# Hash attention and a gated feed-forward on one core: earlier loads, earlier hashes, moves of bits one a slot

## The chip, the cores and the metric

The kernel runs on one core of one Trainium2 chip. The time is the device time of one execution in microseconds. Five engines work side by side, each through its own list of instructions in order: TensorE (PE, and PEld for its weight loads), VectorE (DVE), ScalarE (ACT), GpSimd (POOL) and SyncE (SP), which here only issues transfers. An engine whose next instruction must wait holds everything behind it.

## What is computed

```python
def _attn_ref(q, k, v, proj):                 # q, k, v: (4, 8, 768, 64) f32; proj: (64, 6)
    q_bits = (np.einsum('bhsd,dk->bhsk', q, proj) > 0).astype(np.int64)
    k_bits = (np.einsum('bhsd,dk->bhsk', k, proj) > 0).astype(np.int64)
    q_bucket = np.sum(q_bits * powers, axis=-1)
    k_bucket = np.sum(k_bits * powers, axis=-1)
    mask = q_bucket[:, :, :, None] == k_bucket[:, :, None, :]
    scores = np.where(mask, scale * np.matmul(q, k.transpose(0, 1, 3, 2)), -1000000000.0)
    attn = softmax(scores)                    # written out in the reference
    return np.matmul(attn, v)

def _moe_ref(x, w_gate, w_val, w_out, rms_g): # x: (3072, 512), the heads side by side
    xn = x / np.sqrt(np.mean(x * x, axis=-1, keepdims=True) + 1e-06) * rms_g
    g = xn @ w_gate                           # 512 x 1536
    silu = g * (1.0 / (1.0 + np.exp(-g)))
    return (silu * (xn @ w_val) @ w_out)      # 1536 x 512
```

A query sees the keys whose six sign bits equal its own. The kernel adds the bits to the contraction: rows 64 to 75 of the tile QK hold them, scaled, so that one matmul gives a score that the exp turns into zero wherever bits differ.

## The kernel before

**Tiles.** The 4 batches are cut into 8 windows of 384 queries (window w is half of batch w // 2), the 8 heads into 4 pairs; "(b, hp)" is pair hp of batch b. For each pair the kernel loads q, k and v, turns q and k so that the head's 64 channels lie on partitions, casts them to f16 into QK, hashes them and writes the bits into QK.

**Slots.** The list SLOTS has 192 entries (window, head, third of the keys). One pass of the last loop is a slot: it issues the two score matmuls of the next slot (`scores(s + 1)`, L319, into one of two buffers s_ps), the exp of the next slot (`probs(s + 1)`, L329, on ScalarE), and what the plan holds for slot s. The first 48 slots take windows 0 and 1 in the order of TURNS, six slots a pair: window 0 pair 0, window 1 pair 0, window 0 pair 1, window 1 pair 1, window 0 pair 2, window 0 pair 3, window 1 pair 2, window 1 pair 3. From slot 48 on come the windows 2 to 7, one head after the other, and beside each of them the feed-forward of an earlier window: window 0's from slot 48.

**The plan.** `at(s, f, ...)` puts a piece of work into slot s. Within a slot the order is by rank, then by the order of the calls of `at`: ranks under 3 go ahead of the slot's exp, the others behind it. The order in which pieces are issued is the order on every engine's list.

**Pieces.**
- `load_rows` (L111) loads one of q, k, v of a pair in rows of 1,536 bytes; `load_blocks` (L121) loads k or q of a later pair as four transfers with 128-byte pieces. Both go through SyncE's queue. The ten buffers of the pool L are shared by all loads. `load_w` (L494) and `load_wo` (L500) bring the weights through GpSimd's queue, two halves each.
- `keep_pair(b, hp, i)` is a turn, four for a pair (k and q of each head): three transposes on TensorE (t_ps, L169), a copy on VectorE (L178), and for q a cast on ScalarE straight from the bank (L180). `casts` follows a slot later on GpSimd (L183), two for k and one for q. Batch 0 and the pairs (1,0) and (1,1) go this way. The others are turned by VectorE, `turn_dve` (L193), eight pieces a pair, one a slot.
- `hash_head` (batch 0, heads 0 to 3) and `hash_heads` (a pair): eight small f32 matmuls (d_ps, L209), the signs on VectorE (L216), then moves of the bits into QK: twelve rows of 384 each, eight blocks for a pair. A move is a VectorE copy (L250 for a head, L268 for a pair) or a transfer issued by SyncE (L248, L266). A block has a number t: t = 0 and 1 are k and q of the first half of the queries and keys, t = 2 and 3 those of the second. Pairs (1,2) and later are hashed by `hash_pairs` (L284).
- `attn_out` (rank 4.5, three slots after a pair's last exp): VectorE adds a constant to o_ps, the only buffer of its kind (otmp, L356), takes reciprocals (rcp, L361), GpSimd scales (x, L365) and squares (sq, L377); `sumsq` (L381) six slots later sums on VectorE.
- `norm`, `scale_x`, `turn_x` make the normalised, turned x of a window: ss (L388) on VectorE, ms and rstd (L390, L394) on GpSimd, xn (L399) on VectorE, transposes on TensorE (x_ps, L406) and the product with the gains on VectorE (xnT, L407). For window 0 these stand in slots 39, 41 and 45 to 47, and the first gate matmuls (g_ps, L418) in slot 48.

**When what is due.** A pair's bits and casts must be in QK one slot before its first slot: (0,2) and (0,3) in slots 23 and 29 for window 0, and 35 and 41 for window 1; (1,0) in slot 47, (1,1) in slot 53. In the kernel before, turns, hash and moves of a pair stand like this: (0,2) turns in slots 9, 10, 12, 13, hash in 14; (0,3) in 16, 17, 19, 20, hash in 21; (1,0) in 23, 25, 26, 28, hash in 29; (1,1) in 34, 36, 38, 41, hash in 42. VectorE's four moves of a batch-0 pair follow its signs at once, and so do the three of heads 2 (slot 3) and 3 (slot 7). Pair (1,2) is loaded in slots 29 (v), 31 (k) and 34 (q), and turned from slot 44 on.

Of the kernel before, what the change touches and what calls it, by code (L numbers as in the profile page):

```python
# [43 lines left out]
def kernel(  # L44
# [12 lines left out]
    nc = tc.nc  # L57
# [79 lines left out]
    def t0(b, h, which):  # L137
        hp, hh = divmod(h, 2)
        return T0[b, hp, which][:, hh * HALF : (hh + 1) * HALF]
# [66 lines left out]
    def hash_bank(parts):  # L206
        ps = bank("d_ps", [128, HALF])
        for t, (w, src) in enumerate(parts):
            nc.tensor.matmul(  # L209
                ps[32 * t : 32 * t + 32, :], w, src,  # L210
                start=True, stop=True, tile_position=(0, 32 * t),
            )
        return ps

    def signs(bt, ps, n=128):
        nc.vector.tensor_scalar(  # L216
            out=bt[0:n], in0=ps[0:n], scalar1=thr[0:n], scalar2=scl[0:n],
            op0=ALU.is_gt, op1=ALU.mult,
        )

    def bit_rows(b, h, t):
        return QK[b, h // 2][D:KROWS, h % 2, t * HALF : (t + 1) * HALF]
# [3 lines left out]
    def bits_tile(i):  # L226

        if i % 2 == 0:
            held.append(spool.tile([128, S], FP16, name="bits", bufs=3))
        return held[-1][:, (i % 2) * HALF : (i % 2 + 1) * HALF]  # L230

    def hash_head(h):


        kt, qt = t0(0, h, "k"), t0(0, h, "q")
        ps = hash_bank(
            [(pk[:, 0:32], kt), (pq[:, 0:32], qt), (pk[:, 12:44], kt), (pq[:, 12:44], qt)]
        )
        bt = bits_tile(h)
        signs(bt, ps)  # L240

        def move(movers, t0=0):
            for t, eng in enumerate(movers, t0):
                src = bt[32 * t : 32 * t + 12]
                if eng is nc.scalar:
                    nc.scalar.copy(bit_rows(0, h, t), src)
                elif eng is nc.sync:
                    nc.sync.dma_start(out=bit_rows(0, h, t), in_=src)  # L248
                else:
                    eng.tensor_copy(bit_rows(0, h, t), src)  # L250

        return move

    def hash_heads(b, hp, eng=nc.sync):

        ps = hash_bank(
            [(w[:, 0:32], t0(b, 2 * hp + hh, which))
             for hh in range(2) for w, which in ((pk, "k"), (pq, "q"))]
        )
        bt = bits_tile(0)  # L260
        signs(bt, ps)
        for hh, t in [(0, 2), (1, 2), (0, 0), (0, 1), (1, 0), (1, 1), (0, 3), (1, 3)]:
            p0 = 64 * hh + 32 * (t % 2) + 12 * (t // 2)
            dst, src = bit_rows(b, 2 * hp + hh, t), bt[p0 : p0 + 12]
            if t > 1 or eng is nc.sync:
                nc.sync.dma_start(out=dst, in_=src)  # L266
            else:
                eng.tensor_copy(dst, src)  # L268

    def hash_pairs(b, hps):  # L270

# [272 lines left out]
    def at(s, f, *a, rank=3):  # L544
        plan[s].append((rank, len(plan[s]), lambda: f(*a)))
# [1 line left out]
    def steps(s):  # L547
        return sorted(plan[s], key=lambda e: e[:2])

    def hash_step(h):  # L550
        hash_head(h)((nc.vector, nc.vector, nc.vector, nc.sync))

    for h in range(2):
        at(1 + h, cast_half, 0, h, "q", 1)
        at(h, (bits0, bits1)[h], (nc.vector,), 3)

    for hp, turns, sv in ((1, (1, 2, 4, 5), 8), (2, (9, 10, 12, 13), 19), (3, (16, 17, 19, 20), 25)):
        for i, s in enumerate(turns):
            at(s, keep_pair, 0, hp, i)
            at(s + 1, casts, 0, hp, i)  # L560
        at(sv, v_prep, 0, hp)
    at(3, hash_step, 2)
    at(7, hash_step, 3)
    at(14, hash_heads, 0, 2, nc.vector)
    at(21, hash_heads, 0, 3, nc.vector)
    for hp, s in enumerate((6, 16, 30, 36)):
        at(s, v_mean, 0, hp, 2, range(6))
    for i, (t, src) in enumerate(((wg, moe_w_gate), (wv, moe_w_val))):
        at(2 + 5 * i, load_w, t, src, 0, 768)
        at(13 + 5 * i, load_w, t, src, 768, 1536)  # L570
        at(36 + 5 * i, load_wo, 6 * i, 6 * i + 6)

    for hp, loads, turns, sv in ((0, (9, 11, 16), (23, 25, 26, 28), 30),
                                 (1, (14, 19, 24), (34, 36, 38, 41), 45)):
        for which, s in zip("kqv", loads):
            at(s, load_rows, nc.sync, 1, hp, which)
        for i, s in enumerate(turns):
            at(s, keep_pair, 1, hp, i)  # L580
            at(s + 1, casts, 1, hp, i)
        at(turns[3] + 1, hash_heads, 1, hp)
        at(sv, v_prep, 1, hp)

    work = {
# [121 lines left out]
```

## Time and profile before

| | |
|---|---|
| median of 3 runs | 352.48 us (352.04 to 353.3) |
| the profiled execution | 351.2 us |
| its span, first to last instruction | 349.4 us |
| granted TensorE clock, mean | 0.99 |
| PE busy | 330.6 us (95%) |
| DVE busy | 237.1 us (68%) |
| ACT busy | 209.8 us (60%) |
| POOL busy | 146.6 us (42%) |
| moved by DMA | 31.36 MB, mean 90 GB/s |

The profile lists the time in which each engine was busy, the waits with what ended them, and a chain of work followed back from the last instruction. A busy share is a mean over stages with different limits. This kernel has two: the first 48 slots (about 9.6 to 57 us), in which TensorE makes scores and turns pairs without any feed-forward to fill its time, and the rest. By stretches (us; busy time of each engine, the granted clock, the share of the DMA engines that was busy, GB/s), the first 80 us are:

```profile
core 0: us, PE busy (x) PEld busy (x) DVE busy (x) ACT busy (x) POOL busy (x), PEclk, DMA share, GB/s
0.00:10.00 10.00, 7.87 (x60) 5.78 (x61) 4.78 (x32) 3.49 (x6) 4.17 (x20) 1.00 0.74 231
10.00:20.00 10.00, 9.50 (x96) 5.92 (x96) 7.97 (x19) 8.93 (x14) 7.33 (x12) 1.00 1.11 315
20.00:30.00 10.00, 8.11 (x104) 5.82 (x104) 6.63 (x17) 7.28 (x12) 7.36 (x12) 1.00 1.11 225
30.00:40.00 10.00, 8.41 (x110) 5.83 (x111) 8.52 (x17) 8.73 (x13) 8.58 (x15) 1.00 1.07 263
40.00:50.00 10.00, 9.45 (x124) 6.64 (x125) 5.36 (x12) 9.11 (x14) 8.30 (x14) 1.00 0.18 29
50.00:60.00 10.00, 7.17 (x84) 4.20 (x83) 5.08 (x16) 6.15 (x9) 4.97 (x7) 1.00 1.27 213
60.00:70.00 10.00, 5.48 (x41) 3.10 (x41) 6.15 (x13) 2.85 (x5) 1.64 (x2) 0.66 0.45 68
70.00:80.00 10.00, 10.00 (x87) 5.83 (x86) 8.89 (x21) 5.81 (x10) 4.12 (x5) 1.00 0.90 161
```

Each row says how full the engines are in its ten microseconds, and the third number from the end is the clock that TensorE was granted.

### The profile page before, as it was taken

Reading aid. Unit: us, or ns where it says so; the run is one execution under the profiler, and the core shown is the slowest. Engines: PE = TensorE matmul, PEld = TensorE weight load, DVE = VectorE, ACT = ScalarE, POOL = GpSimd, SP = SyncE. Lnnn points to the kernel's source line nnn. Section 1 sums busy time; section 2 is a strip of 40 time slices with the busy share of each in tenths; the row PEclk is TensorE's granted clock in tenths of the full one; section 3 lists DMA queues with packets and bytes.
Section 4 is the critical chain, followed back from the end, with each engine's and each line's share of the span. In section 5 each row is a group of like instructions: output and inputs, shape, how many; then the busy total and the mean of one; then the engine's idle time right before and its main releaser. Section 6 shows DMA issues by size and latency. Waiting matters only on the chain.

```text
span 349.4 us, 7777 instructions
## 1 busy us (share of the span) xinstructions
PE 330.6 (95%) x2996; PEld 201.7 (58%) x2996; DVE 237.1 (68%) x531; ACT 209.8 (60%) x328; POOL 146.6 (42%) x216
## 2 busy tenths in 40 slices
PE   8898895699999999999999999999999999999995
PEld 6565563356556565566656565566556665555553
DVE  4768663688966797587867797576636663883860
ACT  3888885356566577557766576566767675332331
POOL 4677865143772657621564477513111221110000
PEclk9999999699999999999999999999999999999999
DMA  7999659386284253408345070100010001001002
GB/s 214 350 234 253 139 75 221 50 145 140 43 165 104 57 87 90 106 18 157 73 107 121 16 138 32 62 20 0 19 48 27 3 0 62 32 0 61 32 0 90
DMA packets 80100, 31.36 MB, mean 90 GB/s; under 512 B 65192, under 2 KB 77120, under 8 KB 80064
## 3 DMA queue, kind: packets, MB, share of 16 engines
q1 hardware_dynamic: 76080, 26.09, 30.6%
q0 software_dynamic: 3680, 4.72, 8.3%
q8 instruction: 23, 0.38, 0.5%
q10 hardware_dynamic: 304, 0.07, 0.1%
q14 instruction: 13, 0.11, 0.1%
HBM read 28.32 MB, written 6.29 MB: 99 GB/s over the span
## 4 chain that ended last, share of the span: by engine, by line
PE 82%; DVE 7%; DMA 5%; ACT 3%; issue 1%; SPq 1%; DVEq 0%; ACTq 0%
PE v_ps L428 17%; PE y_ps L442 17%; PE g_ps L418 17%; PE s_ps L319 15%; PE o_ps L341 8%; PE d_ps L209 4%; DMA kL<-in_k_dram 3%; ACT psb L329 2%; PE x_ps L406 1%; DMA qL<-in_q_dram 1%; DVE QK L268 1%; DMA QK<-bits 1%; PE y_ps L666 1%; DVE bits L216 1%; DVE otmp L356 1%
## 5 line engine op out<-in xcount | busy, mean ns | idle before, releaser
L329 ACT ACTIVATE psb<-s_ps 128x768 f16<-128x768 f32 x192 | 150.5, 808 | 31.0 <-PE s_ps L319 29.9
L319 PE MATMUL s_ps<-QK 76*128 76x384 f16 x384 | 93.7, 325 | 4.4 <-ACT psb L329 3.2
L420 ACT ACTIVATE t<-g_ps 128x384 f32<-128x384 f32 x96 | 47.2, 491 | 67.6 <-PE g_ps L418 67.4
L418 PE MATMUL g_ps<-xnT,wg 128*128 128x384 f16 x384 | 78.6, 327 | 7.0 <-DVE xnT L407 7.0
L428 PE MATMUL v_ps<-xnT,wv 128*128 128x384 f16 x384 | 78.7, 327 | 0.4 <-DVE a L430 0.2
L430 DVE SCALAR_TENSOR_TENSOR a<-t,g_ps 128x384 f32<-128x384 f32 x96 | 52.7, 549 | 35.5 <-ACT t L420 33.9
L442 PE MATMUL y_ps<-wo,ht 128*128 128x512 f16 x276 | 69.2, 378 | 0.3 <-DVE a L430 0.3
L365 POOL TENSOR_TENSOR x<-otmp,rcp 128x384 f32<-128x384 f32 x31 | 25.7, 829 | 99.5 <-DVE rcp L361 99.0
L341 PEld LDWEIGHTS <-psb 128*128 128x128 f16 x1152 | 51.9, 97 | 24.2 <-issue 7.4
L431 DVE SCALAR_TENSOR_TENSOR ht<-a,v_ps 128x384 f16<-128x384 f32 x96 | 53.2, 554 | 11.4 <-PE v_ps L428 2.4
L341 PE MATMUL o_ps<-vl,psb 128*128 128x65 f16 x1152 | 56.6, 193 | 1.4 <-DVE otmp L356 1.4
L418 PEld LDWEIGHTS <-wg 128*128 128x128 f16 x384 | 36.0, 97 | 31.2 <-issue 7.6
L428 PEld LDWEIGHTS <-wv 128*128 128x128 f16 x384 | 36.5, 97 | 25.3 <-issue 2.1
L319 PEld LDWEIGHTS <-QK 76*128 76x128 f16 x384 | 31.4, 98 | 22.0 <-issue 8.3
L442 PEld LDWEIGHTS <-ht 128*128 128x128 f16 x276 | 25.8, 97 | 24.1 <-issue 0.5
L449 ACT COPY ysb<-y_ps 128x512 f32<-128x512 f32 x23 | 13.5, 586 | 25.9 <-PE y_ps L442 23.2
L407 DVE TENSOR_TENSOR xnT<-x_ps,gcol 128x512 f16<-128x512 f16 x24 | 16.4, 685 | 15.9 <-PE x_ps L406 15.9
L377 POOL TENSOR_TENSOR sq<-x 128x384 f32<-128x384 f32 x31 | 25.6, 826 | 2.4
L356 DVE TENSOR_TENSOR otmp<-o_ps,cvb 128x390 f32<-128x390 f32 x32 | 17.9, 559 | 11.8 <-PE o_ps L341 11.7
L201 POOL CAST QK<-kT 64x768 f16<-64x768 f32 x20 | 16.4, 821 | 20.0 <-DVE kT L193 12.4
L193 DVE STREAM_TRANSPOSE kT<-kL 128x192 f32<-128x192 f32 x40 | 20.2, 516 | 5.5 <-DMA kL<-in_k_dram 5.5
L201 POOL CAST QK<-qT 64x768 f16<-64x768 f32 x20 | 16.7, 834 | 11.0 <-DVE qT L193 10.4
(74 smaller groups left out, 270.7 us busy)
## 6 DMA issues: line engine op xcount, KB each, us to landing
vL<-in_v_dram SPq DMA_DIRECT2D x16, 384.0 KB
out_dram<-ysb SPq DMA_DIRECT2D x23, 256.0 KB
kL<-in_k_dram SPq DMA_DIRECT2D x40, 96.0 KB
qL<-in_q_dram SPq DMA_DIRECT2D x40, 96.0 KB
kL<-in_k_dram SPq DMA_DIRECT2D x5, 384.0 KB
qL<-in_q_dram SPq DMA_DIRECT2D x5, 384.0 KB
wg<-in_moe_w_gate_dram POOLq DMA_DIRECT2D x2, 768.0 KB, 8.3
wv<-in_moe_w_val_dram POOLq DMA_DIRECT2D x2, 768.0 KB, 9.8
```

What stands on the lines that cost most here:

```text
L201: nc.gpsimd.tensor_copy(QK[b, hp][0:64, hh, o : o + S], T0[b, hp, which][64 * hh : 64 * hh + 64, :])
L319: nc.tensor.matmul(ps[:, j, 0:HALF], k_cols(w // 2, h, 2 * p + j), q_cols(w, h), start=True, stop=True,)
L329: nc.scalar.activation(psb[w, h][:, p], sps.pop(g)[:, :, 0:HALF], AF.Exp, scale=ESCALE,)
L341: nc.tensor.matmul(o[:, c, hh, 0:65], psb[w, h][:, jt // 2, jt % 2, 128 * c : 128 * c + 128], vls[b % 2][:, h, v_chunk(b, h, jt), 0:65], s ...
L365: eng.tensor_mul(xd.rearrange("p c (h d) -> p c h d", h=2), tmp[:, :, :, 0:64], r.to_broadcast([128, 3, 2, 64]),)
L377: nc.gpsimd.tensor_mul(sq, xd, xd)
L418: nc.tensor.matmul(g, wg[:, kt, fs], xnT[w][:, kt], start=(kt == 0), stop=(kt == 3))
L420: nc.scalar.activation(t, g, AF.Tanh, scale=0.5)
L428: nc.tensor.matmul(vv, wv[:, kt, fs], xnT[w][:, kt], start=(kt == 0), stop=(kt == 3))
L430: nc.vector.scalar_tensor_tensor(out=a, in0=t, scalar=1.0, in1=g, op0=ALU.add, op1=ALU.mult)
L431: nc.vector.scalar_tensor_tensor(out=ht[w][:, ft], in0=a, scalar=0.5, in1=vv, op0=ALU.mult, op1=ALU.mult)
L442: nc.tensor.matmul(y, ht[w][:, ft, c * 128 : (c + 1) * 128], wo[:, ft, :], start=(ft == 0), stop=(ft == NF - 1),)
```

## The change

1. Loads: of pair (1,2), k moves from slot 31 to 20, q from 34 to 24, v from 29 to 31; of (1,3), k, q, v from 45, 47, 49 to 36, 40, 46; of (1,0), v from 16 to 15; of (1,1), k, q, v from 14, 19, 24 to 13, 17, 28. Weight loads move by one to three slots, except the first half of the gate.
2. Turns and hashes: (0,2) is turned in slots 8 to 11 and hashed in 13, (0,3) in 13 to 16 and 18, (1,0) in 20, 22, 23, 24 and 26; (1,1)'s hash moves from 42 to 43.
3. Moves of bits: `hash_heads` returns a function that moves given blocks. The batch-0 pairs' odd blocks (t = 2, 3) go to SyncE at once; the four for VectorE stand in slots of their own, 15 to 18 for (0,2) and 19, 21, 22, 23 for (0,3), and those of heads 2 and 3 in the three slots after their hash, all at rank 5, the end of the slot.

```diff
-    def hash_heads(b, hp, eng=nc.sync):
+    def hash_heads(b, hp):
...
-        for hh, t in [(0, 2), (1, 2), (0, 0), (0, 1), (1, 0), (1, 1), (0, 3), (1, 3)]:
-            p0 = 64 * hh + 32 * (t % 2) + 12 * (t // 2)
-            dst, src = bit_rows(b, 2 * hp + hh, t), bt[p0 : p0 + 12]
-            if t > 1 or eng is nc.sync:
-                nc.sync.dma_start(out=dst, in_=src)
-            else:
-                eng.tensor_copy(dst, src)
+
+        def move(eng, blocks):
+            for hh, t in blocks:
+                p0 = 64 * hh + 32 * (t % 2) + 12 * (t // 2)
+                dst, src = bit_rows(b, 2 * hp + hh, t), bt[p0 : p0 + 12]
+                if eng is nc.sync:
+                    eng.dma_start(out=dst, in_=src)
+                else:
+                    eng.tensor_copy(dst, src)
+
+        return move
...
-    def hash_step(h):
-        hash_head(h)((nc.vector, nc.vector, nc.vector, nc.sync))
+    moves = {}
+
+    def hash_one(h):
+        moves[h] = hash_head(h)
+        moves[h]((nc.sync,), 3)
+
+    def hash_pair(b, hp):
+        moves[b, hp] = hash_heads(b, hp)
+        odd = [(0, 2), (1, 2), (0, 3), (1, 3)]
+        even = [(0, 0), (0, 1), (1, 0), (1, 1)]
+        moves[b, hp](nc.sync, odd if b == 0 else even[:2] + odd[:1] + even[2:] + odd[1:])
...
-    for hp, turns, sv in ((1, (1, 2, 4, 5), 8), (2, (9, 10, 12, 13), 19), (3, (16, 17, 19, 20), 25)):
+    for hp, turns, sv in ((1, (1, 2, 4, 5), 8), (2, (8, 9, 10, 11), 19), (3, (13, 14, 15, 16), 25)):
...
-    at(3, hash_step, 2)
-    at(7, hash_step, 3)
-    at(14, hash_heads, 0, 2, nc.vector)
-    at(21, hash_heads, 0, 3, nc.vector)
+
+    for h, s in ((2, 3), (3, 7)):
+        at(s, hash_one, h)
+        for t in range(3):
+            at(s + 1 + t, lambda h=h, t=t: moves[h]((nc.vector,), t), rank=5)
+    for hp, s, slots in ((2, 13, (15, 16, 17, 18)), (3, 18, (19, 21, 22, 23))):
+        at(s, hash_pair, 0, hp)
+        for i, s in enumerate(slots):
+            at(s, lambda hp=hp, i=i: moves[0, hp](nc.vector, [divmod(i, 2)]), rank=5)
...
-        at(2 + 5 * i, load_w, t, src, 0, 768)
-        at(13 + 5 * i, load_w, t, src, 768, 1536)
-        at(36 + 5 * i, load_wo, 6 * i, 6 * i + 6)
+        at(2 + 4 * i, load_w, t, src, 0, 768)
+        at(12 + 5 * i, load_w, t, src, 768, 1536)
+        at(33 + 6 * i, load_wo, 6 * i, 6 * i + 6)
...
-    for hp, loads, turns, sv in ((0, (9, 11, 16), (23, 25, 26, 28), 30),
-                                 (1, (14, 19, 24), (34, 36, 38, 41), 45)):
+    for hp, loads, turns, sv in ((0, (9, 11, 15), (20, 22, 23, 24), 30),
+                                 (1, (13, 17, 28), (34, 36, 38, 41), 45)):
...
-        at(turns[3] + 1, hash_heads, 1, hp)
+        at(turns[3] + 2, hash_pair, 1, hp)
...
-        (1, 2): ((31, 34, 29), 44, 53), (1, 3): ((45, 47, 49), 52, 61),
+        (1, 2): ((20, 24, 31), 44, 53), (1, 3): ((36, 40, 46), 52, 61),
```

## The prediction

> **What bounds the kernel now.** First the page's slices (one digit for 8.7 us, in tenths busy):
>
> ```profile
> PE   8898895699999999999999999999999999999995
> PEclk9999999699999999999999999999999999999999
> ```
>
> TensorE is full from the ninth slice (about 70 us) to the end, so a microsecond is to be had before 70 us or nowhere. The deepest hole, and the only dip of the clock, is in slices 7 and 8 (52 to 70 us). Second, the waits of the first 110 us (total, times, longest, in us):
>
> ```profile
> PE g_ps L418 <- DVE xnT L407: 7.0, 1, 7.0
> DVE kT L193 <- DMA kL<-in_k_dram: 5.5, 1, 5.5
> PE s_ps L319 <- ACT psb L329: 3.2, 6, 1.3
> PE o_ps L341 <- DVE otmp L356: 1.4, 3, 1.1
> ```
>
> Third, VectorE, TensorE and SyncE in order of time (start, duration, idle before it and what ended that):
>
> ```profile
> 55.91 0.19 DVE L361 RECIPROCAL rcp<-otmp 128x6 f32<-128x6 f32 x1
> 61.57 0.52 DVE L193 STREAM_TRANSPOSE kT<-kL 128x192 f32<-128x192 f32 x1 [5.47 <-DMA kL<-in_k_dram]
> ...
> 63.80 0.67 DVE L407 TENSOR_TENSOR xnT<-x_ps,gcol 128x512 f16<-128x512 f16 x1
> ```
>
> ```profile
> 57.02 0.49 PE L319 MATMUL s_ps<-QK 76*128 76x384 f16 x2
> 64.52 1.44 PE L418 MATMUL g_ps<-xnT,wg 128*128 128x384 f16 x4 [7.01 <-DVE xnT L407]
> ```
>
> ```profile
> 41.60 6.08 SPq L266 DMA_DIRECT2D QK<-bits  x8
> 47.78 0.46 SPq L111 DMA_DIRECT2D vL<-in_v_dram  x1
> 48.34 7.13 SPq L121 DMA_DIRECT2D kL<-in_k_dram  x4
> ```
>
> Read upward: the four loads of k of pair (1,2) are issued only at 48.34, because SyncE's queue holds the eight moves of bits of pair (1,0) ahead of them. They land at about 61.5. VectorE's first transpose of that k (slot 44) waits for them, and behind it in VectorE's order stand the three xnT products of window 0, so the first gate matmul starts at 64.52, 7.01 us after TensorE ran dry. The clock pays as well (core's busy times, then clock, DMA share, GB/s):
>
> ```profile
> 57.40:60.40 3.00, 0.11 (x1) 0.00 (x0) 0.00 (x0) 0.20 (x1) 1.35 (x2) 1.00 1.31 209
> 60.50:64.50 4.00, 0.00 (x0) 0.00 (x0) 2.93 (x7) 0.00 (x0) 0.00 (x0) 0.50 0.72 103
> 64.50:67.20 2.70, 2.68 (x9) 1.28 (x9) 0.93 (x2) 1.19 (x2) 1.64 (x2) 0.50 0.06 14
> ```
>
> Ahead of that TensorE works in slots of about 0.99 us (47.4 us from the first to the 49th exp), with smaller holes. Three of them begin behind VectorE's moves of bits; here is the largest:
>
> ```profile
> 33.72 2.52 DVE L268 COPY QK<-bits 12x384 f16<-12x384 f16 x4
> 36.27 0.56 DVE L178 COPY kT<-t_ps 128x384 f32<-128x384 f32 x1
> 36.75 0.55 DVE L178 COPY qT<-t_ps 128x384 f32<-128x384 f32 x1
> ```
>
> ```profile
> 37.33 0.47 ACT L180 CAST QK<-t_ps 64x384 f16<-64x384 f32 x1 [0.97 <-DVE qT L178]
> 38.56 0.48 PE L319 MATMUL s_ps<-QK 76*128 76x384 f16 x2 [1.33 <-ACT psb L329]
> ```
>
> Four moves hold VectorE for 2.52 us, the qT copy is late, ScalarE's cast of the same bank waits for it with the exps queued behind, and TensorE has no free s_ps buffer. The same chain gives 0.66 at 22.49; the moves from 25.54 delay otmp and give 1.06 at 27.56, those from 18.12 another 0.15 at 20.15. Together 3.20 us.
>
> **The change part by part.**
>
> 1. Loads of (1,2): k from slot 31 to 20, q from 34 to 24, so ahead of the eight (1,0) moves on SyncE and behind the four of (0,3). No wait is added: the buffers that they take were read out by slot 16. SyncE ends the (0,3) moves at 36.8 now; three slots earlier is about 33.5. Eight issues at the 0.67 to 0.71 us of L121 in the chain of waits are 5.5 us; their 0.77 MB at the 209 GB/s of the first window row are 3.8 us. Even held up by the weights, as the 13.1 us from 48.34 to landing were, k is there at about 47, against the transpose at 56.1. So VectorE's 5.47 us go: the transpose starts at 56.10 and the third xnT, 2.9 us later as now, ends at 59.0. Gain 5.47. What is late next is that VectorE queue itself: four transposes and three products behind rstd, xn, otmp; TensorE keeps 7.01 - 5.47 = 1.54 us of the hole.
>
> 2. Clock. The last row has 2.70 us at 0.50, worth 1.35 us. It fell three microseconds into the hole; holes of 1.33 us cost no clock. A hole of 1.54 us is nearer to these: gain 1.35, bounds 0 and 1.35.
>
> 3. Moves of bits. The same 14 copies leave VectorE's blocks of three (heads 2, 3: 1.03 and 1.38 us) and four (1.37 and 2.52 us) and stand one a slot, behind the slot's copy and otmp. At most all 3.20 us come back. Against it: the turns of (0,2) and (0,3) now fill slots 8 to 11 and 13 to 16 without a gap. By rows, such a slot costs TensorE 0.33 (scores) + 0.27 (o_ps) + 0.33 (t_ps) and ScalarE 0.73 + 0.38 where it casts, 1.11 us every second slot; slots 17 to 19 get lighter for it, and what is moved all stays ahead of slot 38. POOL's casts come earlier with them: over slots 8 to 25 it has two v casts (0.8), three x with sq (1.66 each), twelve turns' casts (9.3) and two weight issues (0.8), 17.5 us for 18 slots; sums of sq are read six slots later, which leaves it some 2 us. Bounds: +3.20, and -1.33 (nothing regained and one more hole like the largest). I take 2.0, nearer the upper end, as the blocks are what the trace names.
>
> A move lasts 0.25 us alone, but 0.79 and 0.89 at 33.98 and 34.78, each ending with the POOL operation beside it. The Trainium skill (SBUF — State Buffer, "Who interferes with whom") says why: a two-port copy on VectorE and a GpSimd operation exclude each other for the whole instruction. By that, spreading could meet a busier POOL 14 times; its result is rival A.
>
> 4. Hidden edits. The hashes of (0,2), (0,3), (1,0) come 1, 3 and 3 slots earlier, (1,1)'s one later: the same matmuls (0.83 to 0.9 each), two slots behind their last copy. The weight issues on POOL (0.8 to 0.97 us): the second wo in slot 39 stands ahead of ms, where POOL idles 2.02 us today; without this cover it would cost 0.9. Loads of (1,0), (1,1), (1,3) move up on a DMA that carries 12 GB/s from 42 to 48 us. TensorE's 0.3 us wait for bits at 84.75 may go too; counted as nothing.
>
> Sum: 5.47 + 1.35 + 2.0 = 8.8 us. The profiled execution took 351.2 (span 349.4 and 1.8 around it), so 342.4. The median of the runs, 352.48, stands 1.3 above it: 343.7.
>
> **Rivals.**
>
> A. The dense slots give part 3 back: late copies at slots 14 and 22 to 24 hold ScalarE's casts as at 37.33. For it: VectorE is at 8.5 of 10 us in the 30:40 stretch, POOL at 8.6. Against: from 9.1 to 57.5 VectorE is busy 34.4 of 48.4 us. Part 3 becomes -1.33: 352.5 - 5.47 - 1.35 + 1.33 = 347.0. The skill's rule of the shared port leads to the same result. Chance 15%.
>
> B. The hole is bound by something else almost as late: rstd on POOL (52.13 to 53.02) and xn; or (1,1)'s bits, now behind eight loads of (1,3), come late to slot 53. For it: the VectorE queue leaves 1.54 us anyway. Against: both chains move up with the slots. Another 2 us are lost: 345.7. Chance 12%.
>
> C. Slower: (1,0)'s eight moves stand behind the eight loads on SyncE. TensorE needs them at slot 47, about 54 us. In this row the weights' queue leaves q1 almost nothing while three such loads are pending (56 to 60 us: MB, share):
>
> ```profile
> q0 software_dynamic: 738, 0.75, 120.1%
> q1 hardware_dynamic: 455, 0.06, 14.3%
> ```
>
> If the loads wait out the second wv and both wo transfers (8.5 us each, median, from 42 on: about 59.5), the moves (8 x 0.76) land at 66, TensorE stands 12 us at slot 47, and 8.8 - 12 is a loss of 3: 355.7. It turns into a loss once they land after 63. Against: 5 us of free DMA between wv and wo. Chance 5%. The Trainium skill (DMA: Bandwidth & Descriptors, "Queues, rings and completion order") states that each DMA engine serves the queues that have work in turn, a packet from each. By that the loads would keep about half the rate and C could not come about; these two rows do not agree (0.06 MB against 0.75), so C stays.
>
> D. The loads come no earlier in effect, since SyncE is late in reaching them, and only part 3 counts: 350.5. Against: 20 us lie between. Chance 3%.
>
> **How the numbers follow.** Forecast 65%, 343.7, its own range 341 to 346. The lower end of all is 352.5 - 5.47 - 1.35 - 3.20 - 1.54 = 340.9, with the residual hole gone too; the upper takes A and B together, 347.0 + 2 = 349, cut to 348.5. Within 0.3% (1.1 us, what a measurement can tell from none): 3%, D's milder half and mixtures; slower: 7%, C and what I have overlooked; faster: 90%.
>
> **What would show it.** Right: no VectorE idle on kL; the first gate at about 57, after a hole of 1 to 2 us; no slice of PEclk under 9; the 49th exp near 55; moves one at a time. Wrong: a hole over 3 us before the first gate, TensorE waiting on QK<-bits near slots 47 or 53 or on kL at slot 20, or the 49th exp still at 57.

## The result and the profile after

| | before | after |
|---|---|---|
| median (4 runs each) | 352.68 us (352.04 to 353.3) | 346.62 us (346.31 to 348.44) |
| ratio, 95% interval | | 0.9839 [0.98, 0.9878] |
| the profiled execution | 351.2 us | 346.73 us |
| its span | 349.4 us | 345.0 us |
| granted clock, mean | 0.99 | 1.0 |

The kernel became 6.1 us faster by the medians and 4.47 us between the two profiled executions. The forecast was 343.7 us (8.8 us less), range 341.0 to 348.5: the direction and the range hold, and about half of the forecast gain is missing in the traces. The two differences do not agree because the profiled execution of before lies 1.5 us under its median and that of after does not lie under its own.

The slices of the kernel after (tenths busy, one digit for 8.6 us):

```profile
PE   7889897996999999999999999999999999999995
PEclk9999999999999999999999999999999999999999
```

The clock has no slice under 9 any more, and the seventh and eighth slices rose from 5 and 6 to 7 and 9. A new dip stands in the tenth (78 to 86 us), which was full before. The waits of the kernel after in its first 110 us (total, times, longest) say what it is:

```profile
PE s_ps L323 <- DMA QK<-bits: 3.6, 2, 3.3
PE s_ps L323 <- ACT psb L333: 3.3, 7, 0.9
PE g_ps L422 <- DVE xnT L411: 1.5, 1, 1.5
...
PE o_ps L345 <- DVE otmp L360: 0.4, 2, 0.2
```

VectorE's wait on kL is not in the list at all, and the wait before the first gate fell from 7.0 to 1.5. The line at the top is new: score matmuls that wait for moves of bits. TensorE of the kernel after, in order of time (start, duration, idle before it and what ended that):

```profile
55.97 0.49 PE L323 MATMUL s_ps<-QK 76*128 76x384 f16 x2
58.00 0.81 PE L422 MATMUL g_ps<-xnT,wg 128*128 128x384 f16 x4 [1.54 <-DVE xnT L411]
...
66.17 0.48 PE L323 MATMUL s_ps<-QK 76*128 76x384 f16 x2 [0.29 <-DMA QK<-bits]
...
80.44 0.48 PE L323 MATMUL s_ps<-QK 76*128 76x384 f16 x2 [3.32 <-DMA QK<-bits]
```

The first gate starts at 58.00 instead of 64.52, after a hole of 1.54 us instead of 7.01. Then TensorE waits 0.29 us for the bits of pair (1,1) at slot 54, and 3.32 us for those of (1,2) at slot 60. VectorE of the kernel after shows what is left of the first hole, and when the signs of (1,2) are ready:

```profile
54.86 0.19 DVE L365 RECIPROCAL rcp<-otmp 128x6 f32<-128x6 f32 x1
55.03 0.52 DVE L193 STREAM_TRANSPOSE kT<-kL 128x192 f32<-128x192 f32 x1
...
57.29 0.66 DVE L411 TENSOR_TENSOR xnT<-x_ps,gcol 128x512 f16<-128x512 f16 x1
...
68.13 1.31 DVE L216 TENSOR_SCALAR bits<-d_ps,thr,scl 64x384 f16<-64x384 f32 x2 [1.00 <-PE d_ps L209]
```

The transpose of kL starts right behind the reciprocal. The third xnT ends at 57.95, and the gate follows. The signs of (1,2) are ready at 69.44, eleven microseconds before TensorE gets the bits. SyncE's queue holds them for the first eight of these, until 77.40; the rest is the transfer. The kernel after:

```profile
52.07 7.63 SPq L121 DMA_DIRECT2D kL<-in_k_dram  x4
59.80 3.34 SPq L121 DMA_DIRECT2D qL<-in_q_dram  x4
63.25 6.63 SPq L268 DMA_DIRECT2D QK<-bits  x8
69.99 0.46 SPq L111 DMA_DIRECT2D vL<-in_v_dram  x1
70.56 2.80 SPq L121 DMA_DIRECT2D kL<-in_k_dram  x4
73.45 3.84 SPq L121 DMA_DIRECT2D qL<-in_q_dram  x4
77.40 3.18 SPq L288 DMA_DIRECT2D QK<-bits  x4
```

And the kernel before:

```profile
61.53 6.22 SPq L266 DMA_DIRECT2D QK<-bits  x8
67.86 5.81 SPq L121 DMA_DIRECT2D kL<-in_k_dram  x8
73.76 2.66 SPq L121 DMA_DIRECT2D qL<-in_q_dram  x4
76.52 0.59 SPq L111 DMA_DIRECT2D vL<-in_v_dram  x1
77.21 2.85 SPq L121 DMA_DIRECT2D qL<-in_q_dram  x4
80.18 3.66 SPq L284 DMA_DIRECT2D QK<-bits  x4
```

In both kernels SyncE issues without a pause through this stretch. Before, it came to the bits of (1,2) at 80.18, and TensorE got them at 84.75 after a wait of 0.25 us. The slack there was zero: SyncE, not the hash, set that moment. After, TensorE is ready for slot 60 at 77.12, 7.38 us earlier, but SyncE comes to these bits only 2.78 us earlier. (The hole is smaller than the difference of 4.60, because from their issue to the scores it took 4.57 us before and 3.04 after.) The reason is in the lines above. The change moved the loads of (1,3) from slots 45 and 47 to 36 and 40, and so ahead of the bits of (1,1). Its k takes 7.63 us to issue there, and the bits of (1,1) go out at 63.25, which is later than the 61.53 of the kernel before, although TensorE is ahead of the kernel before (exp 48 by 1.05 us, and the first gate by 6.52).

### The profile page after: what moved, and what is told of

It is laid out like the page before. It is cut to its first block, busy times and chain, and to the rows that moved or that the text cites. A ratio compares the mean times of both kernels' runs of the same rounds, so it can differ in the third digit from the quotient of the medians.

```text
span 345.0 us, 7777 instructions
## 1 busy us (share of the span) xinstructions
PE 327.9 (95%) x2996; PEld 200.3 (58%) x2996; DVE 236.7 (69%) x531; ACT 209.6 (61%) x328; POOL 147.1 (43%) x216
## 4 chain that ended last, share of the span: by engine, by line
PE 82%; DVE 8%; ACT 4%; DMA 2%; issue 2%; SPq 0%; POOL 0%; DVEq 0%; ACTq 0%; POOLq 0%
PE y_ps L446 17%; PE v_ps L432 17%; PE g_ps L422 17%; PE s_ps L323 15%; PE o_ps L345 9%; PE d_ps L209 4%; ACT psb L333 3%; PE x_ps L410 1%; PE t_ps L169 1%; DMA kL<-in_k_dram 1%; DVE otmp L360 1%; DMA QK<-bits 1%; DVE ssp L385 1%; DVE a L434 1%; PE y_ps L684 1%
```

## Where the 4.47 us come from

The start of a slot's exp, counted from exp 0, tells how far the kernel has come: exp 8 stands at 17.56 before and 17.61 after, exp 48 at 56.78 and 55.73, exp 72 at 105.25 and 100.93. From exp 72 to the end of the span all kernels of this study take 244.0 to 244.2 us, so the whole difference lies ahead of it.

| stretch | before | after | difference |
|---|---|---|---|
| exp 8 to 48 | 39.22 | 38.12 | -1.10 |
| exp 48 to 72 | 48.47 | 45.20 | -3.27 |

The second row by its parts: 5.47 us of the first hole are gone, as are 1.38 of the clock (the first gate group took 1.44 us for what takes 0.81, and the rest of the stretch ran at 0.50 to 67.29); 3.36 came in with the bits (3.32 and 0.29, less the 0.25 of before). That is -3.49 against the measured -3.27. The first row is mostly the spread moves with the dense turns: it grows in slots 8 to 16 (7.97 to 9.23 us) and shrinks in slots 24 to 38 (13.57 to 11.72). The last 0.22 of it are not theirs. Slots 38 to 48 take 9.18 us in the kernel before and in e6 and e12, which have the weights wo at their old slots, and 8.93 to 8.95 in after, e1 and e11, which have them early. So the moves and turns gave 0.88 us (39.22 to 38.34) and the early wo the rest. In the lists of waits, the two lines that the moves can touch went from 3.2 and 1.4 us to 3.3 and 0.4: the wait on otmp went, the one behind ScalarE's exps stayed.

The largest of the holes that are left, in the kernel after. VectorE, then ScalarE:

```profile
33.48 0.58 DVE L270 COPY QK<-bits 12x384 f16<-12x384 f16 x1
34.09 0.56 DVE L178 COPY qT<-t_ps 128x384 f32<-128x384 f32 x1
```

```profile
34.68 0.47 ACT L180 CAST QK<-t_ps 64x384 f16<-64x384 f32 x1 [0.86 <-DVE qT L178]
```

It is the chain of the kernel before with one move in place of four: the move ends at 34.06, beside GpSimd's x (33.12 to 33.95); the qT copy is late, ScalarE's cast waits 0.86 us, and TensorE has no free s_ps for 0.94.

## The experiments

All twelve, with the two stretches of each profiled execution (us). Ratios are to the kernel before as it was run beside each of them.

| run | median | ratio, 95% interval | exp 8 to 48 | 48 to 72 |
|---|---|---|---|---|
| before | 352.68 | 1 | 39.22 | 48.47 |
| after | 346.62 | 0.9839 [0.98, 0.9878] | 38.12 | 45.20 |
| e1_q20_behind_bits | 343.90 | 0.9747 [0.9718, 0.9776] | 38.09 | 41.50 |
| e11_13_back | 342.66 | 0.9719 [0.9681, 0.9756] | 38.10 | 41.50 |
| e6_wo_and_13_back | 343.53 | 0.9735 [0.9693, 0.9777] | 38.34 | 41.50 |
| e12_wo_back | 349.01 | 0.9887 [0.9853, 0.9921] | 38.34 | 47.44 |
| e3_loads_alone | 347.56 | 0.9852 [0.9804, 0.99] | 44.71 | 41.51 |
| e4_all_but_loads | 351.54 | 0.9957 [0.9933, 0.9981] | 42.09 | 48.19 |
| e9_moves_in_blocks | 346.32 | 0.983 [0.9809, 0.985] | 40.04 | 41.50 |
| e8_sparse_turns | 343.84 | 0.9758 [0.9736, 0.9781] | 39.66 | 41.79 |
| e2_turn_12_early | 344.55 | 0.9786 [0.9763, 0.981] | 41.93 | 39.02 |
| e7_wo_13_back_turn_early | 346.08 | 0.9826 [0.9799, 0.9854] | 42.14 | 39.81 |
| e10_turn_36_hash_50 | 344.62 | 0.977 [0.9741, 0.98] | 40.94 | 41.01 |
| e13_turn_12_late | 348.86 | 0.9915 [0.9894, 0.9937] | 38.11 | 48.00 |

### Is the new hole SyncE's order?

**e1_q20_behind_bits**, from the kernel after: the load of q of (2,0) goes from slot 51 to 55, behind the hash of (1,2).

```
-        (2, 0): ((46, 51, 54), 58, None),
+        (2, 0): ((46, 55, 54), 58, None),
```

> Only the loads of q of pair (2,0) move, from slot 51 to 55, behind the moves of the bits of (1,2). Theory (SyncE's queue makes the new hole): the first bits of (1,2) are issued some 3.8 us earlier, the hole of 3.32 us before the scores of slot 60 shrinks to under 0.5, median 343.3 to 343.8, ratio to before about 0.975. Rival (the bits are late from VectorE's signs or from landing): the hole stays over 2.5 us and the median at 346 to 347.

Measured: 343.90 us. The bits of (1,2) go out at 74.13 and no score matmul waits for bits; slots 48 to 72 take 41.50, 3.70 less than after (3.32 + 0.29 are 3.61). Moving one load of q, with no change of what is computed or moved, gives it back. The hole of 3.32 is the order on SyncE, shown. The 0.29 at slot 54 went for another reason: this execution was 1.02 us later by exp 48 (56.75), while SyncE issued the bits of (1,1) only 0.55 later (63.80).

**e6_wo_and_13_back**, **e11_13_back** and **e12_wo_back** ask who made SyncE late, the loads of (1,3) or the two weight issues of wo. e6 puts both back where they were before; e11 puts back the loads alone, e12 the wo alone.

```
-        at(33 + 6 * i, load_wo, 6 * i, 6 * i + 6)       # e6, e12
+        at(36 + 5 * i, load_wo, 6 * i, 6 * i + 6)
-        (1, 3): ((36, 40, 46), 52, 61),                 # e6, e11
+        (1, 3): ((45, 47, 49), 52, 61),
```

> The changed kernel with both halves of wo back in slots 36 and 41 and the loads of (1,3) back in 45, 47, 49. Theory (the bits of (1,1) and then of (1,2) are late because the (1,3) loads stand on SyncE behind two weight transfers in a row): the bits of (1,1) are issued before 60 instead of from 63.3 on, and the hole before the scores of slot 60 shrinks to under 1.5 us, median 344 to 345.5. Rival (SyncE has the same number of issues to make before those bits in either order): the hole stays within 1 us of 3.3 and the median at 346 to 347.

> The changed kernel with the loads of (1,3) alone back in 45, 47, 49 (wo as changed). Theory (the eight loads of (1,3) ahead of the bits of (1,1) are what keeps SyncE late): bits of (1,1) issued from about 53, those of (1,2) by 74, no hole before slot 60, median 343.3 to 344.3. Rival (two transfers of wo in a row are the cause): the hole stays over 2 us, median 345.5 to 347.

> The changed kernel with wo alone back in 36 and 41 ((1,3) early as changed). Theory (the loads of (1,3) ahead of the bits of (1,1) are the cause): with the weights later still, the loads wait longer, the bits of (1,1) go out after 63, hole before slot 60 of 3 us or more, perhaps one at slot 54 too, median 346.5 to 349. Rival (wo in a row is the cause): no hole over 1 us, median 343.5 to 344.5.

Measured: 343.53, 342.66 and 349.01 us. SyncE's queue in e11:

```profile
53.75 6.11 SPq L268 DMA_DIRECT2D QK<-bits  x8
59.97 5.79 SPq L121 DMA_DIRECT2D kL<-in_k_dram  x8
...
72.41 3.16 SPq L288 DMA_DIRECT2D QK<-bits  x4
```

With the loads of (1,3) behind them, the bits of (1,1) go out at 53.75 instead of 63.25, those of (1,2) at 72.41 instead of 77.40, and no score matmul waits for bits. k of (1,3) and (2,0), eight issues, take 5.79 us here; in the kernel after, the four of (1,3) alone took 7.63. In e12, with wo at its old slots and the loads of (1,3) early, the holes are about as in the kernel after or longer (0.90 us at slot 54 and 3.30 at slot 60), and the clock pays as well. TensorE at slot 60, and then the core's busy times of the stretch behind it, with the clock in the column behind POOL's:

```profile
82.22 0.48 PE L323 MATMUL s_ps<-QK 76*128 76x384 f16 x2 [3.30 <-DMA QK<-bits]
```

```profile
83.50:86.90 3.40, 3.40 (x20) 1.93 (x17) 1.87 (x6) 1.25 (x3) 1.94 (x4) 0.50 0.94 202
```

So the early loads of (1,3) are the cause, and the early wo is not. Early and late wo are not told apart by the times, neither with these loads early (346.62 and 349.01, but the intervals of the ratios overlap, and part of the difference is the clock) nor with them late (342.66 and 343.53). **e11 has the lowest median: 0.9719 [0.9681, 0.9756], clearly ahead of both kernels.** It is not told apart from e1, e6, e8 and e10, whose intervals overlap its own. Its slack is small: from the first issue of these bits to the scores that wait for them the kernel after and e12 took 3.04 us, so an estimate for e11's bits is 75.45, and its scores of slot 60 start at 75.88.

### Do the parts of the change need each other?

**e3_loads_alone**, from the kernel before: only the loads of (1,2) move.

```
-        (1, 2): ((31, 34, 29), 44, 53),
+        (1, 2): ((20, 24, 29), 44, 53),
```

> The kernel before with k and q of (1,2) loaded in slots 20 and 24 and nothing else changed. Theory (the first two terms of the prediction come from this edit alone): no wait on kL, first gate at about 59.0 after a hole of 1.5 us, clock full throughout; 352.7 - 5.5 - 1.35 = 345.8 if the bits of (1,2) are in time, up to 347.5 if they make a hole again. Rival (it needs the earlier hashes and turns too): a wait on kL of over 2 us stays, or TensorE waits for the bits of (1,0), and the median is above 349.

Measured: 347.56 us (346.28 to 349.52, of which 349.52 is the profiled one). The wait on kL is gone, and the hole before the first gate is 1.55 us. But TensorE now waits at slot 31, the second of pair (0,3) for window 0, for bits of that pair. SyncE and TensorE of e3:

```profile
30.61 12.02 SPq L121 DMA_DIRECT2D kL<-in_k_dram  x4
42.72 3.16 SPq L266 DMA_DIRECT2D QK<-bits  x4
```

```profile
44.81 0.50 PE L319 MATMUL s_ps<-QK 76*128 76x384 f16 x1 [3.47 <-DMA QK<-bits]
```

Their hash is still in slot 21 here, so the load issued in slot 20 stands ahead of them and takes 12.02 us to issue. This is the mechanism that the prediction's rival C put at (1,0)'s bits, one pair earlier. The clock in this execution fell to 0.51 from 45 to 50 us. The four executions of e3 fall into two kinds: 346.28 and 346.58 at a mean clock of 1.0, and 348.53 and 349.52 at 0.990 and 0.989, so the clock is the two or three microseconds between them.

**e4_all_but_loads**, from the kernel after: the loads of (1,2) go back, everything else stays.

```
-        (1, 2): ((20, 24, 31), 44, 53),
+        (1, 2): ((31, 34, 31), 44, 53),
```

> The changed kernel with k and q of (1,2) back in slots 31 and 34. Theory: the first 38 slots gain 1.0 us as in the changed kernel, the hole before the first gate comes back, though shorter, since the bits of (1,0) go through SyncE three slots earlier: 4 to 7 us, clock halved again, median 349.5 to 351.7. Rival (the prediction's 2.0 us for the moves, or more, was there and the profiled run hides it): the 38th slot more than 1.8 us earlier than before.

Measured: 351.54 us (349.45 to 354.21 in ten runs). The profiled execution is the longest of the ten, so its sizes are an upper end; its mean clock is 0.976, and TensorE waits for bits 4.6 us in two places: 3.16 at slot 60, as in the kernel after, and 1.42 at slot 31, for bits of (0,3). SyncE and TensorE of e4 at slot 31:

```profile
31.64 14.23 SPq L268 DMA_DIRECT2D QK<-bits  x12
```

```profile
42.43 0.50 PE L323 MATMUL s_ps<-QK 76*128 76x384 f16 x1 [1.42 <-DMA QK<-bits]
```

The first of these twelve moves are the bits of (0,3), issued at 31.64 with no load of (1,2) ahead of them. So here it is not the order on SyncE that is late but the transfer, by almost eleven microseconds; why is not shown. The hole before the first gate came back at 2.09 us, under the 4 to 7 that were expected. All the rest of the change without the early load is worth about 1.4 us of the 6.1. The two parts do not add up: early loads alone 5.4 (353.0 to 347.6), all the rest 1.4, and both 6.1. Each part alone makes the bits of (0,3) late at slot 31, in e3 behind a load and in e4 on the way.

### What is the spread of the moves worth?

**e9_moves_in_blocks**, from e6: VectorE's moves stand in a block behind the signs again, with the dense turns kept.

```
-            at(s + 1 + t, lambda h=h, t=t: moves[h]((nc.vector,), t), rank=5)
+            at(s, lambda h=h, t=t: moves[h]((nc.vector,), t))
...
-        for i, s in enumerate(slots):
-            at(s, lambda hp=hp, i=i: moves[0, hp](nc.vector, [divmod(i, 2)]), rank=5)
+        for i in range(4):
+            at(s, lambda hp=hp, i=i: moves[0, hp](nc.vector, [divmod(i, 2)]))
```

> The version with wo and (1,3) back, with VectorE's moves of bits again in blocks of three and four behind their signs, turns and hashes in their new slots. Theory (prediction: the blocks hold late copies and otmp): exps 0 to 47 longer than 45.5 us by 1 to 2 us, median 344.5 to 345.5. Rival (the spread is worth nothing, the first 48 slots are set by TensorE's and ScalarE's work in the slots): within 0.4 us of 45.5, median 343.2 to 343.9.

Measured: 346.32 us against e6's 343.53, intervals apart, the medians differing by 2.8 us. From exp 8 to 48 the spread is worth 1.70 us of it; of the profiled executions' difference another 1.24 stand ahead of exp 0, where the two kernels do the same. TensorE's waits in e9 that e6 has not, or has smaller (its otmp wait is 0.6):

```profile
PE o_ps L345 <- DVE otmp L360: 1.8, 4, 0.6
...
PE m_ps L310 <- ACT QK L180: 1.4, 1, 1.4
```

The longest stands behind a block of four moves, `26.73 2.03`, on VectorE: the same chain as before the change. Against it, the wait behind ScalarE's exps is shorter in e9 (2.3 us) than in e6 (3.3).

**e8_sparse_turns**, from e6: the other half, moves one a slot but turns and hashes at their old slots, but (1,0)'s hash one later, in slot 30 (the load of k of (1,2) in slot 22, behind the hash of (0,3)).

```
-    ... (2, (8, 9, 10, 11), 19), (3, (13, 14, 15, 16), 25)):
+    ... (2, (9, 10, 12, 13), 19), (3, (16, 17, 19, 20), 25)):
-    for hp, s, slots in ((2, 13, (15, 16, 17, 18)), (3, 18, (19, 21, 22, 23))):
+    for hp, s, slots in ((2, 14, (15, 16, 17, 18)), (3, 21, (22, 23, 24, 25))):
-    ... (0, (9, 11, 15), (20, 22, 23, 24), 30),
+    ... (0, (9, 11, 15), (23, 25, 26, 28), 30),
-        (1, 2): ((20, 24, 31), 44, 53),
+        (1, 2): ((22, 24, 31), 44, 53),
```

> The version with wo and (1,3) back, with the turns of (0,2), (0,3), (1,0) in their old slots (9, 10, 12, 13; 16, 17, 19, 20; 23, 25, 26, 28), hashes in 14, 21, 30, k of (1,2) loaded in 22, moves of bits one a slot. Theory (the dense turns take back what the spread moves bring): exps 0 to 47 shorter than 45.5 us by 0.5 or more, about 44.5 to 45.0, so median 342.5 to 343.1. Rival (the dense turns cost nothing on balance, as what they add in slots 8 to 16 is missing later): exps 0 to 47 within 0.3 us of 45.5, median 343.3 to 343.8.

Measured: 343.84 us, not told apart from e6. From exp 8 to 48 it takes 39.66, with one hole of 1.26 us at slot 31, for bits of (0,3), which the dense kernels e6, e11 and after have not. SyncE and TensorE of e8:

```profile
33.27 3.06 SPq L268 DMA_DIRECT2D QK<-bits  x4
```

```profile
40.11 0.34 PE L323 MATMUL s_ps<-QK 76*128 76x384 f16 x1 [1.26 <-DMA QK<-bits]
```

The bits went out ahead of the load (issued from 36.44), and the scores still started 6.84 us later. Without the hole the stretch takes 38.40, as e6's 38.34, so the dense turns cost nothing here on balance (1.0 us more in slots 8 to 16, as much less later). What they buy is time for these bits: e6 issues them at 30.48, and no score matmul waits. With the moves in blocks the dense turns are not even: e9 takes 40.04 where the kernel before takes 39.22. So the spread is worth 0.8 us with the old turns and 1.7 with the dense ones.

### Can the 1.54 us before the first gate go?

VectorE's order in that stretch, four transposes of kL among three xnT, suggests that (1,2) turned at another time would free it. **e2_turn_12_early** does this from the kernel after, **e7_wo_13_back_turn_early** from e6 (turned from slot 36, hashed in 45); **e10_turn_36_hash_50** from e6 with the hash in 50; **e13_turn_12_late** from e11, with both later (48 and 57).

```
-        (1, 2): ((20, 24, 31), 44, 53),
+        (1, 2): ((20, 24, 31), 36, 45),      # e2, e7
+        (1, 2): ((20, 24, 31), 36, 50),      # e10
+        (1, 2): ((20, 24, 31), 48, 57),      # e13
```

> The changed kernel with pair (1,2) turned from slot 36 (was 44) and hashed in 45 (was 53). Theory (the hole before the first gate that is left, 1.54 us, is VectorE's queue of four transposes among the three xnT products; the hole of 3.32 us before slot 60 is SyncE's order): the transposes lie in slots 36 to 43 where VectorE idles, the bits of (1,2) stand ahead of the loads of (2,0), first gate hole under 0.6, no hole before slot 60, median 341.8 to 342.8. Rival (rstd and xn hold the gate anyway, or q of (1,2), landed at about 46 us, now holds VectorE in slot 40): the gate hole stays over 1.2 us or a new one comes before slot 48, median 343.3 or more.

> Both: wo and the loads of (1,3) back as before, and (1,2) turned from slot 36, hashed in 45. Theory: without the hole at slot 60 already, only the gate hole shrinks, by about 1 us: median 342.3 to 342.9 against 343.5 of the version without the early turn. Rival (what VectorE does earlier slows the first 48 slots by as much): 343.5 or more, exps 0 to 47 longer by 0.8 us.

> Wo and the loads of (1,3) back, (1,2) turned from slot 36 but hashed only in 50. Theory (in the version hashed in 45 TensorE stood 1.2 us because the hash came before VectorE's last q transpose): that wait goes, the gate hole stays at 0.2 as there, median 342.0 to 343.0 against 343.5 of the version turned from 44. Rival (VectorE's eight transposes in slots 36 to 43 push rstd and xn back by what they take, so the first gate is no earlier): median 343.5 or more.

> The version with the loads of (1,3) back, and pair (1,2) turned from slot 48 (was 44), hashed in 57 (was 53). Theory (the 1.54 us before the first gate are the three k transposes that stand among the xnT products): the hole falls by three transposes of 0.4 us to 0.3 to 0.5, first gate 1.1 us earlier, and SyncE, busy with loads until about 72 anyway, issues the bits of (1,2) no later than 73: median 341.3 to 342.3 against 342.7. Rival (two pairs' transposes in slots 52 to 55 and the later hash take it back): TensorE waits on VectorE or on the bits between slots 50 and 60 by 1 us or more, median 342.7 or more.

Measured: 344.55, 346.08, 344.62 and 348.86 us. The wait before the first gate did fall: to 0.2 us in e2 and e7, to under what the list shows in e10, to 0.41 in e13. None beats e11, whose two stretches sum to 79.60 us against 80.95, 81.95, 81.95 and 86.11 (only the sum tells, since the hash of (1,2) moves between the stretches). In e2 and e7 the hash comes too soon behind VectorE's last transposes: d_ps waits for qT, 1.20 and 1.35 us; in e7 v_ps also waits 1.1 us for VectorE. In e10 the place is taken by another pair of engines. VectorE and GpSimd of e10:

```profile
52.01 2.79 DVE L403 TENSOR_SCALAR xn<-x,rstd 128x512 f16<-128x512 f32 x3 [0.22 <-POOL rstd L398]
```

```profile
51.95 1.78 POOL L201 CAST QK<-kT 64x768 f16<-64x768 f32 x2
```

The three xn take 2.79 us beside these casts; in the kernel before, after, e11 and e13 they take 1.60 to 1.77 (and in e2 and e7, turned as early, 2.65 and 2.80). otmp is late behind them, TensorE waits 1.75 us for it, and the clock is at 0.50 from 56.8 to 60.1 us. In e13 SyncE takes it back. TensorE and SyncE of e13:

```profile
80.47 0.80 PE L323 MATMUL s_ps<-QK 76*128 76x384 f16 x2 [5.51 <-DMA QK<-bits]
```

```profile
72.91 4.39 SPq L121 DMA_DIRECT2D kL<-in_k_dram  x4
77.41 0.83 SPq L288 DMA_DIRECT2D QK<-bits  x1
```

The first gate came at 55.91, 1.46 us earlier than in e11 (57.37), of which 0.33 were there before exp 48, so the hole is indeed the transposes among the xnT. But slots 54 and 56 put v of (2,0) and k of (2,1) on SyncE ahead of a hash in slot 57: the signs are ready at 73.77, the bits go out at 77.41, and TensorE waits 5.51 us, with the clock at 0.50 from 77.4 to 84.1 us. A version with this hash late and those loads behind it was not tried.

## Why the prediction was right in direction and off in size

By the medians the forecast of 343.7 us was 2.9 us too low; between the profiled executions, 342.4 against 346.73, 4.3 us. The measured 346.62 lies in the whole range but above the forecast's own, 341 to 346: the upper end that holds it was made from the rivals A and B.

**Part 1, the loads, 5.47 us: right to the hundredth.** The wait on kL is gone, the hole fell from 7.01 to 1.54, and the residual is the queue that was named, four transposes and three products (e13 takes them apart and the hole goes to 0.41). That the loads come early enough was right, but "no wait is added" holds only because the same change hashes (0,3) sooner; e3, without that, waits 3.47 us for those bits. The estimate of k landing at about 47 at the latest left open how long SyncE is held while it issues: the eight issues, 5.5 us in the sum, took 5.81 and 4.00.

**Part 2, the clock, 1.35: right** (1.38), in the profiled execution, and in part by luck. The reason given, that a hole of 1.54 us is near holes that cost no clock, does not hold in general: with the hole of 1.42 us in e4 the clock is at 0.50 from 42.1 to 48.9 us, and with that of 1.75 in e10 for 3.3 us.

**Part 3, the moves, 2.0: mis-sized; it was 0.88,** without the 0.22 of the early wo. The part was taken nearer to the upper end, 3.20. The wait on otmp fell by 1.0, but the one behind ScalarE's exps did not (3.2 and 3.3), since one move beside a GpSimd operation still makes the qT copy late. The mean of a pair's moves (L268, then L270) fell from 477 to 392 ns and did not come to 0.25 us. Of the 13 moves of L250 only the six of heads 2 and 3 were spread, and these did: from blocks of 1.03 and 1.38 us to five moves of 0.25 and one of 0.37. The prediction's sentence on the shared port of VectorE and GpSimd (the Trainium skill, SBUF — State Buffer, "Who interferes with whom") pointed that way, and the rows agree: 0.58 us for the move at 33.48, 2.79 for the xn of e10. Of the two halves of this part, the spread gained (e9) and the dense turns were even (e8).

**Part 4, the hidden edits, at nothing: the step that failed.** It says of the wait at 84.75 that it "may go too; counted as nothing". A wait of 0.25 us at a place where a queue arrives just in time is no small gain to come. It says that the slack is zero, so every microsecond that TensorE gains ahead of it must be gained by SyncE too. And in the sum the loads of (1,0), (1,1) and (1,3) were weighed only by the DMA's bandwidth, not by the queue that issues them; that queue stands in the prediction only as rival B, for slot 53. With them ahead of (1,1)'s bits, SyncE gained 2.78 us where TensorE gained 7.38, and 3.36 us went to the two waits for bits. e1 gives the larger one back, e11 both. In the other direction, the earlier wo, counted at nothing too, came with a gain of 0.22.

**The sum.** 5.47 + 1.38 + 0.88 + 0.22 - 3.36 = 4.59, against 4.47 between the profiled executions. The forecast added 1.3 us to reach the median from the profiled execution; after the change the profiled execution is the median within 0.1, which gave that much back. The eleven runs of the kernel before beside e2 show one reason: the five at a mean clock of 0.990 have a median of 351.73, the six at 0.984 and 0.985 one of 352.75, and the profiled execution of before had 0.990.

**The rivals.** A (the dense slots take part 3 back) held in a third: part 3 lost 1.1 of its 2.0, not 3.3, and not through the dense slots, which are even by e8. B named bits that come late, those of (1,1) behind the loads of (1,3): that happened, at 0.29 us, and the rest of the same delay came out one pair later at 3.32. Its price, 2 us, was too small because it stopped at slot 53. C (a loss, (1,0)'s bits behind the loads) did not come about at (1,0): those bits went out from 44.16 to 50.33 and no score matmul waited. Its mechanism is that of e3, where it cost 3.47 us. The two rows that it rests on were set against each other by bytes, 0.75 and 0.06 MB; by packets they read 738 and 455, much nearer to taking turns packet by packet than the prediction says (from 52 to 54 us of the kernel after they are 340 and 68, so the doubt stays). D did not happen.

**What would show it.** No idle on kL, the first gate near 57 (58.00), no slice of PEclk under 9, the 49th exp near 55 (55.73): all came. "TensorE waiting on QK<-bits" was listed as a sign of error near slots 47 and 53; it came at 53 and, larger, at 59 to 60.

## What to carry to other kernels

A queue that issues transfers is an engine with an order of its own: when a load is moved up, list what it is moved ahead of on that queue, and what waits for each of these. A wait of a few tenths on a transfer in the trace of before says that the slack there is gone; ask what that queue must issue by then, and whether it gets faster by as much as the work in front. Loads that are needed late belong behind the small moves that are needed soon, even if the DMA seems free.

## What the runs showed of the hardware

**Issuing the same four small-piece loads took from 2.80 to 12.02 us.** Four loads of k in 128-byte pieces took 2.80 us to issue in the kernel after at 70.56, 7.63 at 52.07 and 12.02 in e3. From 52 to 54 us of the kernel after, the weights' queue moved 0.35 MB and the queue of these loads 0.03; from 56 to 58 it is 0.11 against 0.54. In e3 it is not the weights alone: from 31 to 35 us the loads' own queue moved 1.08 MB and the weights' 0.02, from 35 to 39 it is 0.23 against 0.67. What holds the issuing itself is not shown.

**The clock falls near the start of some executions, with TensorE busy.** The same stretch in e6 and in e11 (clock in the column behind POOL's):

```profile
10.50:14.00 3.50, 3.50 (x17) 1.36 (x16) 1.30 (x3) 2.25 (x4) 3.32 (x6) 0.51 1.07 377
```

```profile
10.50:14.00 3.50, 3.50 (x24) 1.75 (x24) 2.48 (x6) 3.22 (x5) 3.16 (x6) 1.00 1.07 385
```

Slots 0 to 8 took 8.59 us in e6 and 7.45 in e11, though the edits between them come later than that; the same in e1 (8.60) and e12 (8.63). So part of a microsecond between two single executions of this kernel may be the clock of its first slots; not all of it, since the kernel after took 8.13 us there at a clock of 1.00.

**The length of a hole does not tell whether the clock falls.** A hole of 3.3 us before slot 60 left the clock at 1.00 in the profiled execution of the kernel after and took it to 0.50 for 3.4 us in that of e12; in e3 a hole of 3.47 us goes with a mean clock of 0.99 in the profiled execution, and half of e3's executions kept 1.0. Behind shorter holes it fell too, 1.42 us in e4 and 1.75 in e10, while 1.54 in the kernel after and 1.26 in e8 left it at 1.00. What decides is open.
